# Two copies of an unpacked weight given out later, and Grams, D and lane copies of the steady pairs moved by half a slot or more

## The chip, the cores and the metric

The kernel runs on one core of a Trainium2 chip. The metric is the device time of one launch, in microseconds; lower is better. A core has five engines, each with a queue of its own that it works off in order: TensorE (PE; its weight loads are listed apart as PEld), VectorE (DVE), ScalarE (ACT), GpSimd (POOL) and SyncE (SP, which here only issues DMAs). An instruction starts when its engine comes to it and the semaphores that it waits for have been reached.

## What is computed

The reference is a linear attention by the delta rule, followed by a feed-forward layer. Per batch and head (4 x 8), over 768 steps, with a state matrix of 48 x 48:

```python
for t in range(S):
    y[:, :, t] = np.einsum('bhd,bhde->bhe', q[:, :, t], state)
    v_old = np.einsum('bhde,bhd->bhe', state, kt)
    state = state + bt[:, :, :, None] * np.einsum('bhd,bhe->bhde', kt, vt - v_old)
...
h = x @ w_in
g = np.where(pos, h, np.where(neg, 0.0, (h + beta) ** 2 / (4.0 * beta)))
return (g @ w_out).astype(np.float32)
```

k is normalised, y of the heads side by side is x (3072 tokens x 384), w_in is 384 x 2048 and w_out 2048 x 384; beta of the feed-forward is 1, and pos and neg mean h >= 1 and h <= -1.

## The kernel before

**Chunks and pairs.** The 768 steps are cut into 12 chunks of 64. Two chunks make a pair, so there are 6 pairs, G = 0 to 5. A chunk g is worked on in these pieces, each of them a function that issues matmuls, returns a function that copies the result out (the eviction), and that may return a third part for VectorE:

- `gram(g, i)` (four per chunk): products of keys with keys and of keys with queries, from the loaded tile W. ScalarE copies the first into GG (L150), VectorE masks the second back into W (L163); for the first four chunks ScalarE copies it (L155) and POOL masks it.
- `lanes`: from GG of both chunks, 32 x 32 triangular blocks, one per lane: two generator steps of two copies each (L202), one for each chunk, a transposition (L204), and the norms with gm, ending in the scaling L217 and POOL's mask L218 and memset L220.
- `solve_whole`: 30 steps of two VectorE operations each (L247, L249) that invert the blocks; `unlanes_whole` puts them back (L255, L257, L260). For pairs 0 and 1 `solve` and `unlanes` do it in blocks of 16 (L236, L238, L268 to L272) and `merge16_a` and `merge16_b` put them together.
- `merge32_a` (L308), `merge32_b` (L324): TensorE joins the blocks to 64 x 64. `scale_v` (L184, one VectorE operation for each half of a chunk) multiplies the values by the norm.
- `chain_r` (L338), `chain_u` (L352), `chain_y` (L372), `chain_d` (L396): the chunk's use of the state, its update, its output (split into a high and a low part, L377 to L382, and sent on by six DMAs, L386) and the addition to the state (L407, four VectorE operations). These run chunk after chunk.

**The feed-forward.** For each pair, 16 slices f of the hidden width: `up` (L522, nine matmuls: three slices of the model width times three products of high and low parts), then on ScalarE a Relu from h, a second Relu and a Square (L644, L644, L663), and the max on VectorE (L671); in the next slot's beginning the cast to a high part on ScalarE (`ghi`, L639) and the low part on VectorE (`glo`, L640); two slots later `down` (L537, twelve matmuls). One slice is one slot. Pair 0 has 24 slots (8 of half the tokens, 8 of all, 8 of the other half), the others 16, so 104 in all. `h` has two buffers: an up waits for the max of two slots before. `ch`, which takes the results of the small pieces, has two buffers as well.

**Order.** The order of all instructions is written out by hand. In a slot n come: what is left of the last slot's second half (its evictions); ghi and glo of the last slot; up; first Relu; the pieces that are planned for time n (products); one step of the weight generator `wu`; the fills planned for n; the evictions; another step of `wu`; second Relu, Square; down; the pieces planned for n + 0.5; the max; two steps of `wu`; the fills for n + 0.5. `plan(G)` fills two tables, `pe` for pieces and `fill` for generators and loads, counted from the pair's first slot; a = 2G + 2 and b = 2G + 3 are the chunks of the next pair, whose lanes, solve, merges and chain run beside this pair's feed-forward, while Grams and loads of the pair after it stand near the pair's end. T is 5 for G = 0 and 1 for the steady pairs G = 1 to 4. So in a steady pair chain_y(b) is given out at 14.5, load_w(b + 2) at 15, Grams of a + 2 at 15 and 15.5, of b + 2 at 15.5 and 16, chain_d(b) at 17, which is slot 1 of the next pair, and load_kv(b + 2) at 17.5. W and KV have four buffers, two chunks: load_w(b + 2) has to wait until chain_y(b) has read W, load_kv(b + 2) until chain_d(b) has read KV.

**The weights.** They come as 64-bit words and are unpacked once, tile by tile (16 tiles f), by the generator `weight(f)`, in six steps: a scaling copy on ScalarE (L125), a shift on VectorE (L127), two bit operations on VectorE (L129, L131), the cast to the high part on ScalarE (L135) and the low part on VectorE (L137). `unpack` interleaves the tiles, and each `yield` of it is one step of `wu`: 26 are used before the first slot, then four per slot until slot 9. Four buffers (`X4`) hold the tile in work.

Of the kernel before, what the change touches and what calls it, by code (L numbers as in the profile page):

```python
# [20 lines left out]
FT = DF // 128  # L21
# [8 lines left out]
def delta_rule_moe(ctx: ExitStack, tc: tile.TileContext, kqa, kqb, kv, beta, w, out):  # L30
# [89 lines left out]
    def weight(f):  # L120

        x = X4[:, f % 4]
        st = RAW.pop(f)
        sti, xi = st.bitcast(I32), x.bitcast(I32)
        nc.scalar.mul(out=x, in_=st[:, :, 1::2], mul=2.0 ** -112)  # L125
        yield
        nc.vector.tensor_scalar(out=xi, in0=xi, scalar1=3, scalar2=None, op0=ALU.logical_shift_left)  # L127
        yield
        nc.vector.scalar_tensor_tensor(out=xi, in0=sti[:, :, 1::2], scalar=-0x80000000, in1=xi, op0=ALU.bitwise_and, op1=ALU.bitwise_or)  # L129
        yield  # L130
        nc.vector.scalar_tensor_tensor(out=xi, in0=sti[:, :, 0::2], scalar=29, in1=xi, op0=ALU.logical_shift_right, op1=ALU.bitwise_or)  # L131
        yield
        WT[f] = const.tile([P, 2, 2, DM], F32R, name=f"wt{f}")
        hi, lo = (WT[f][:, :, i, :] for i in range(2))
        nc.scalar.copy(out=hi, in_=x)  # L135
        yield
        nc.vector.tensor_tensor(out=lo, in0=x, in1=hi, op=ALU.subtract)  # L137
        yield


    def gram(g, i):

        w_, us = W[g, i // CT], [i % CT * NP + p for p in range(NP)]
        gp = ps.tile([P, NP, 2, C], F32, **acc())
        for p, u in enumerate(us):
            nc.tensor.matmul(gp[0:C, p], w_[C:C + D, 0, u, :], w_[C:C + D, 0:2, u, :], start=True, stop=True)  # L146
            nc.tensor.matmul(gp[C:P, p], w_[0:D, 0, u, :], w_[0:D, 0:3:2, u, :], start=True, stop=True)  # L147

        def evict():
            nc.scalar.copy(out=GG[:, g % 2, i * NP:(i + 1) * NP], in_=gp[:, :, 0, :])  # L150

            def raw():
                for r, s in ((0, 1), (C, 2)):
                    x = w_[r:r + C, s, us[0]:us[0] + NP]
                    nc.scalar.copy(out=x, in_=gp[r:r + C, :, 1, :])  # L155
                    nc.gpsimd.affine_select(out=x, in_=x, pattern=[[0, NP], [1, C]], base=0, channel_multiplier=-1,
                                            compare_op=ALU.is_gt, fill=0.0)
            if g < 4:
                return raw

            def masks():
                for r, s in ((0, 1), (C, 2)):
                    nc.vector.tensor_tensor(out=w_[r:r + C, s, us[0]:us[0] + NP], in0=gp[r:r + C, :, 1, :],  # L163
                                            in1=mask[r:r + C, None, :].broadcast_to([C, NP, C]), op=ALU.mult)
            return masks
        return evict
# [13 lines left out]
    def scale_v(g):  # L180

        for i in range(NT):
            v, u = KV[g, i][:, 1], g % 2 * NU + i * NV
            nc.vector.tensor_tensor(out=v, in0=v, in1=S["N"][:, u:u + NV, None].broadcast_to([P, NV, D]), op=ALU.mult)  # L184
            yield
# [44 lines left out]
    def solve():  # L230

        X, A16 = S["X"], S["A16"]
        for j in range(15):
            n, m = j + 1, 15 - j
            pr = sb.tile([P, 240], F32, name="pr", bufs=1)[:, 0:2 * n * m].rearrange("l (s c t) -> l s c t", s=2, t=m)
            nc.vector.tensor_tensor(out=pr, in0=X[:, :, 0:n, j:j + 1].broadcast_to([P, 2, n, m]),  # L236
                                    in1=A16[:, :, j:j + 1, j + 1:16].broadcast_to([P, 2, n, m]), op=ALU.mult)
            nc.vector.tensor_tensor(out=X[:, :, 0:n, j + 1:16], in0=X[:, :, 0:n, j + 1:16], in1=pr, op=ALU.subtract)  # L238
            yield
# [177 lines left out]
    def products(*pieces):  # L417
        return [p() for p in pieces]

    def both(f, g):  # L420
        return [lambda i=i: f(g, i) for i in range(NT)]
# [6 lines left out]
    def unpack():  # L428

        gens = [weight(f) for f in range(FT)]  # L430

        def step(f):
            if f < FT:
                next(gens[f])
        step(0)
        step(1)
        for f in range(FT + 2):
            if f < FT:
                step(f)
                yield  # L440
            if f > 1:
                step(f - 2)
                yield
            step(f + 2)
            if f < FT:
                step(f)
                yield
                step(f)
                step(f)
                yield  # L450


    def stage(pieces, *fill):
# [4 lines left out]

    spare += START
    wu, sv, ln, raws = unpack(), [scale_v(0), scale_v(1)], lanes(0), []  # L460
    for g in range(2):
        for i in range(CB):
# [84 lines left out]
    pe, fill = {}, {}  # L547

    def at(where, G, t, *x):
        where.setdefault(2 * first[G] + int(round(2 * t)), []).extend(x)  # L550

    def grams(G, t, g, dt=0.5):
        for j in range(2):
            at(pe, G, t + j * dt, *[lambda i=2 * j + x: gram(g, i) for x in range(2)])

    def plan(G):

        a, b = 2 * G + 2, 2 * G + 3
        if G < NS - 1:
            ln, so, un, va, vb = lanes(G + 1), solve(), unlanes(), scale_v(a), scale_v(b)  # L560
        if G == 0:
            at(pe, G, 0, *both(chain_y, 1))
            at(fill, G, 1, (load_w, 3))
            at(pe, G, 1, *both(chain_d, 1))
            at(fill, G, 1.5, (load_kv, 3))
            grams(G, 2, a)
            grams(G, 4, b)
            at(fill, G, 4, (ln, 1))
            at(fill, G, 5, (ln, 1))
            at(fill, G, 5.5, (ln, 1))  # L570
            at(fill, G, 6, (ln, 9))
            for j in range(8):
                at(fill, G, 6.5 + j / 2, (so, 2))
            at(fill, G, 9, (va, 1))
            at(fill, G, 9.5, (va, 1))
            at(fill, G, 10.5, (un, 1))
            at(fill, G, 11, (un, 9))
            at(fill, G, 13, (vb, 1))
            at(fill, G, 14, (vb, 1))
            T = 5  # L580
        elif G < NS - 1:
            so, un = solve_whole(), unlanes_whole()
            for j in range(2):
                at(fill, G, 2 + j, (va, 1))
                at(fill, G, 11 + j, (vb, 1))
            at(fill, G, 0.5, (ln, 2))
            at(fill, G, 1, (ln, 1))
            at(fill, G, 1.5, (ln, 9))
            cost, H = 0, 0
            for j in range(1, 31):  # L590
                at(fill, G, 2.5 + H / 2, (so, 1))
                cost += j * (31 - j) + 150
                H = int(cost / 9461 * 14)
            for j in range(4):
                at(fill, G, 9.5 + j // 2 / 2, (un, 1))
            T = 1
        if G < NS - 1:
            if G == 0:
                for j, f in enumerate((merge16_a, merge16_b, merge32_a, merge32_b)):
                    for g in range(2):  # L600
                        at(pe, G, T + 7 + j + g / 2, lambda f=f, g=g: f(g))
            else:
                for j, f in enumerate((merge32_a, merge32_b)):
                    for g in range(2):
                        at(pe, G, 10.5 + j + g / 2, lambda f=f, g=g: f(g))
            at(pe, G, T + 6.5, *both(chain_r, a))
            at(pe, G, T + 11, *both(chain_u, a))
            at(pe, G, T + 11.5, *both(chain_y, a))
            at(pe, G, T + 12, *both(chain_d, a))
            at(pe, G, T + 12.5, *both(chain_r, b))  # L610
            at(pe, G, T + 13, *both(chain_u, b))
            at(pe, G, T + 13.5, *both(chain_y, b))
            if G < NS - 2:
                at(fill, G, T + 12, (load_w, a + 2))
                at(fill, G, T + 12.5, (load_kv, a + 2))
                late = 0 if G == 0 else 2
                at(pe, G, T + 14 + late, *both(chain_d, b))
                at(fill, G, T + 14, (load_w, b + 2))
                at(fill, G, T + 14.5 + late, (load_kv, b + 2))
                grams(G, T + 14 + (G == 0) / 2, a + 2)  # L620
                grams(G, T + 14.5 + (G == 0), b + 2)

    for G in range(NS):
        plan(G)
# [21 lines left out]
    late, last, ready = [], None, []  # L646
    for n, item in enumerate(items):
# [22 lines left out]
        late = products(*pe.pop(H + 1, []))  # L670
# [6 lines left out]
    G = NS - 1  # L677
# [50 lines left out]
```

## Time and profile before

| | us |
|---|---|
| three runs | 716.6, 718.3, 722.27 (median 718.3) |
| profiled execution, its own time | 714.19 |
| its span, first to last instruction | 712.2 |
| TensorE's granted clock, mean of the span | 0.944 |

In the profile, times count from the first instruction. The stretch before the first slot ends near 80 us, pair 0's slots lie between 80 and 230, the steady pairs 1 to 4 take some 97 to 106 us each (the first up of pairs 2, 3 and 4 stands near 328, 432 and 537), and pair 5, which has only its feed-forward, begins near 634. A group of instructions is named by its line, its engine and its tiles (out<-in); "idle before" is the time in which the engine had nothing running ahead of it, and the arrow names what ended that time.

### The profile page before, as it was taken

To read this page: it belongs to the slowest core of one execution; us is meant where nothing else is said; L and a number is where in the kernel's file an instruction comes from. 1 tells how busy PE (TensorE), PEld (TensorE's weight loads), DVE (VectorE), ACT (ScalarE), POOL (GpSimd) and SP (SyncE) were. 2 spreads that over 40 slices of the span, in tenths; PEclk is the share of its full clock that TensorE was granted. 3 is DMA by queue.
4 is the path that set the end of the run, shared out by engine and by line. 5 is a ranking of instruction groups with operands and counts; after the bars stand their busy time and mean duration, and the time that the engine had idled before them with its cause. 6 is when DMAs were issued, how large, how long until landed. Compare 5 with 4: busy or idle time off the path is not lost.

```text
span 712.2 us, 19365 instructions
## 1 busy us (share of the span) xinstructions
PE 646.0 (91%) x8428; PEld 558.4 (78%) x8428; DVE 440.7 (62%) x920; ACT 400.1 (56%) x720; POOL 45.1 (6%) x90
## 2 busy tenths in 40 slices
PE   8848776679999899998999999999989999999996
PEld 7348775468898788887888878888878888889985
DVE  2857667894255798346996445996436996433332
ACT  3327666454845565844467653457554467556663
POOL 3212022001000200000200000200000200000000
PEclk9955988799999999999999998999998999999999
DMA  8960430000053000042300150300150200001001
GB/s 235 417 252 9 118 99 1 0 1 5 3 137 103 23 1 1 5 112 59 89 1 2 34 121 20 88 2 2 39 133 10 83 1 2 14 13 44 1 1 45
DMA packets 18532, 41.45 MB, mean 58 GB/s; under 512 B 3600, under 2 KB 9104, under 8 KB 18448
## 3 DMA queue, kind: packets, MB, share of 16 engines
q1 hardware_dynamic: 18112, 40.04, 19.5%
q8 instruction: 66, 1.08, 0.6%
q14 instruction: 18, 0.15, 0.1%
q0 software_dynamic: 256, 0.08, 0.1%
q10 hardware_dynamic: 80, 0.10, 0.1%
HBM read 33.13 MB, written 4.72 MB: 53 GB/s over the span
## 4 chain that ended last, share of the span: by engine, by line
PE 47%; DVE 33%; ACT 6%; issue 5%; DMA 4%; SPq 3%; DVEq 0%; ACTq 0%
PE h L522 15%; PE o L537 14%; DVE pr L247 5%; DVE A L249 4%; DVE s L671 4%; DVE glo L640 4%; DMA W<-in_kqa_dram 3%; PE ch L372 3%; PE ch L352 3%; SPq L386 2%; PE ch L146 2%; PE ch L324 2%; PE ch L396 2%; PE ch L308 2%; PE ch L338 2%
## 5 line engine op out<-in xcount | busy, mean ns | idle before, releaser
L522 PE MATMUL h<-xb,wt 128*128 128x512 f32 (+1 forms) x936 | 231.8, 393 | 13.6 <-DVE s L671 11.4
L522 PEld LDWEIGHTS h<-xb,wt 128*128 128x128 f32 x936 | 167.9, 194 | 52.2 <-DVE s L671 16.6
L537 PE MATMUL o<-wt,ghi 128*128 128x384 f32 x768 | 202.0, 344 | 2.4 <-ACT ghi L639 2.4
L537 PEld LDWEIGHTS o<-wt,ghi 128*128 128x128 f32 x768 | 138.1, 189 | 11.6 <-ACT ghi L639 3.0
L671 DVE TENSOR_TENSOR s<-h,s 128x512 f32<-128x512 f32 (+1 forms) x104 | 66.9, 643 | 113.9 <-ACT s L663 113.8
L537 PE MATMUL o<-wt,glo 128*128 128x384 f32 x384 | 131.6, 343 | 2.4 <-DVE glo L640 2.1
L639 ACT CAST ghi<-s 128x512 fp32r<-128x512 f32 (+1 forms) x104 | 61.1, 588 | 94.5 <-DVE s L671 68.6
L644 ACT ACTIVATE s<-h,half 128x512 f32<-128x512 f32 (+1 forms) x104 | 67.9, 653 | 56.7 <-PE h L522 56.3
L640 DVE TENSOR_TENSOR glo<-s,ghi 128x512 fp32r<-128x512 f32 (+1 forms) x104 | 67.3, 647 | 44.6 <-ACT ghi L639 44.2
L537 PEld LDWEIGHTS o<-wt,glo 128*128 128x128 f32 x384 | 72.6, 189 | 6.0 <-DVE glo L640 6.0
L644 ACT ACTIVATE s<-s,one 128x512 f32<-128x512 f32 (+1 forms) x104 | 71.9, 691 | 2.9
L663 ACT ACTIVATE s<-s 128x512 f32<-128x512 f32 (+1 forms) x104 | 62.3, 599 | 3.3
L146 PE MATMUL ch<-W 48*64 48x128 f32 x336 | 47.8, 300 | 17.7 <-DMA W<-in_kqa_dram 7.0
L146 PEld LDWEIGHTS ch<-W 48*64 48x64 f32 x336 | 42.3, 150 | 23.4 <-issue 13.9
L147 PE MATMUL ch<-W 48*64 48x128 f32 x336 | 48.0, 300 | 0.0
L163 DVE TENSOR_TENSOR W<-ch,mask 64x256 f32<-64x256 f32 x64 | 27.0, 422 | 32.6 <-ACT GG L150 31.7
L249 DVE TENSOR_TENSOR A<-A,pr 128x30 f32<-128x30 f32 (+14 forms) x120 | 39.8, 332 | 4.4
L147 PEld LDWEIGHTS ch<-W 48*64 48x64 f32 x336 | 42.2, 150 | 0.0
L247 DVE TENSOR_TENSOR pr<-A 128x30 f32<-128x30 f32 (+14 forms) x120 | 39.3, 328 | 2.2
L150 ACT COPY GG<-ch 128x256 f32<-128x256 f32 x42 | 15.2, 372 | 37.2 <-PE ch L147 37.1
L218 POOL TENSOR_SCALAR_AFFINE_SELECT A<-A 128x1024 f32<-128x1024 f32 x4 | 6.4, 1593 | 370.4 <-DVE A L217 370.4
L135 ACT CAST wt<-xb 128x768 fp32r<-128x768 f32 x16 | 13.3, 832 | 28.9 <-DVE xb L131 28.9
(137 smaller groups left out, 721.1 us busy)
## 6 DMA issues: line engine op xcount, KB each, us to landing
wt<-in_w_dram SPq DMA_DIRECT2D x16, 768.0 KB, 13.7
KV<-in_kv_dram SPq DMA_DIRECT2D x24, 384.0 KB, 5.5
W<-in_kqb_dram SPq DMA_DIRECT2D x24, 256.0 KB, 4.7
W<-in_kqa_dram SPq DMA_DIRECT2D x24, 192.0 KB, 4.9
out_dram<-wx SPq DMA_DIRECT2D x47, 96.0 KB, 2.2
xb<-X SPq DMA_DIRECT2D x66, 32.0 KB, 2.0
xb<-A SPq DMA_DIRECT2D x6, 32.0 KB, 2.0
beta_sb<-in_beta_dram POOLq DMA_DIRECT2D x8, 10.0 KB, 2.4
```

The source lines that it names most:

```text
L146: nc.tensor.matmul(gp[0:C, p], w_[C:C + D, 0, u, :], w_[C:C + D, 0:2, u, :], start=True, stop=True)
L147: nc.tensor.matmul(gp[C:P, p], w_[0:D, 0, u, :], w_[0:D, 0:3:2, u, :], start=True, stop=True)
L163: nc.vector.tensor_tensor(out=w_[r:r + C, s, us[0]:us[0] + NP], in0=gp[r:r + C, :, 1, :], in1=mask[r:r + C, None, :].broadcast_to([C, NP, ...
L247: nc.vector.tensor_tensor(out=pr, in0=A[:, 0:n, j:j + 1].broadcast_to([P, n, m]), in1=A[:, j:j + 1, j + 1:32].broadcast_to([P, n, m]), op= ...
L249: nc.vector.tensor_tensor(out=A[:, 0:n, j + 1:32], in0=A[:, 0:n, j + 1:32], in1=pr, op=ALU.add)
L522: nc.tensor.matmul(h[:, cols(bs)], WT[f][:, 0, x, k * P:(k + 1) * P], XB[G][:, y, k, cols(bs)], start=(n == 0), stop=(n == 8))
L537: nc.tensor.matmul(oacc[G, k], (ghi, glo)[x][:, k * P:(k + 1) * P], WT[f][:, 1, y, :], start=(new and n == 0), stop=(left[G, b] == 0 and n ...
L639: nc.scalar.copy(out=ghi[:, c], in_=s[:, c])
L640: nc.vector.tensor_tensor(out=glo[:, c], in0=s[:, c], in1=ghi[:, c], op=ALU.subtract)
L644: nc.scalar.activation(out=out, in_=in_, func=AF.Relu, bias=bias, scale=scale)
L663: nc.scalar.activation(out=s[:, c], in_=s[:, c], func=AF.Square)
L671: nc.vector.tensor_tensor(out=s[:, c], in0=h[:, c], in1=s[:, c], op=ALU.max)
```

## The change

Two edits. In `unpack`, the step that makes the high part of tile f (L135, together with the second bit operation in one step of `wu` before) is taken one tile later, ahead of the second bit operation of tile f + 1; and the scaling copy of tile f + 2 (L125), which stood ahead of the first bit operation of f, comes behind the last step of f.

In `plan`, for the steady pairs:

- scale_v of chunk a: from 2 and 3 to 4 and 5;
- lanes: from two steps at 0.5, one at 1, the rest at 1.5, to one step each at 0.5, 1 and 1.5 and the rest at 2;
- chain_d(b) from 17 to 15, load_kv(b + 2) from 17.5 to 15.5 (G = 1 to 3);
- Grams of b + 2 from 15.5 and 16 to 16 and 16.5 (G = 1 to 3).

chain_r(a) is written in another place with the same times (11.5 for G = 0, 7.5 for the steady pairs), and G = 0 keeps its times. Number and size of all instructions stay.

```diff
@@ -441,13 +441,15 @@
             if f > 1:
                 step(f - 2)
                 yield
-            step(f + 2)
             if f < FT:
                 step(f)
                 yield
-                step(f)
+            if 0 < f <= FT:
+                step(f - 1)
+            if f < FT:
                 step(f)
                 yield
+            step(f + 2)
...
@@ -581,11 +583,12 @@
             for j in range(2):
-                at(fill, G, 2 + j, (va, 1))
+                at(fill, G, 4 + j, (va, 1))
                 at(fill, G, 11 + j, (vb, 1))
-            at(fill, G, 0.5, (ln, 2))
+            at(fill, G, 0.5, (ln, 1))
             at(fill, G, 1, (ln, 1))
-            at(fill, G, 1.5, (ln, 9))
+            at(fill, G, 1.5, (ln, 1))
+            at(fill, G, 2, (ln, 9))
...
         if G < NS - 1:
+            at(pe, G, 11.5 if G == 0 else 7.5, *both(chain_r, a))
...
-            at(pe, G, T + 6.5, *both(chain_r, a))
...
@@ -613,12 +617,11 @@
-                late = 0 if G == 0 else 2
-                at(pe, G, T + 14 + late, *both(chain_d, b))
+                at(pe, G, T + 14, *both(chain_d, b))
                 at(fill, G, T + 14, (load_w, b + 2))
-                at(fill, G, T + 14.5 + late, (load_kv, b + 2))
+                at(fill, G, T + 14.5, (load_kv, b + 2))
                 grams(G, T + 14 + (G == 0) / 2, a + 2)
-                grams(G, T + 14.5 + (G == 0), b + 2)
+                grams(G, T + 15 + (G == 0) / 2, b + 2)
```

## The prediction

> **What bounds the kernel now.** I read the page first (busy shares), then busy time by stretches, then the timelines of single engines in the two stretches that the edits touch, and the chain of work that ended last for the joints between pairs.
>
> ```profile
> PE 646.0 (91%) x8428; PEld 558.4 (78%) x8428; DVE 440.7 (62%) x920; ACT 400.1 (56%) x720; POOL 45.1 (6%) x90
> 80.00:158.00 78.00, 54.28 (x435) 45.71 (x435) 59.30 (x119) 44.96 (x92) 9.97 (x21) 0.80 0.15 39
> 441.00:489.00 48.00, 46.62 (x386) 40.52 (x386) 45.63 (x106) 26.39 (x42) 3.83 (x6) 1.00 0.12 34
> ```
>
> TensorE looks like the bound at 91%, but not everywhere. In 80 to 158 us, where pair 0's feed-forward starts and the weights are still unpacked, it works 54 of 78 us and part of that at a low clock (0.80 mean); VectorE works 59, ScalarE 45, and neither is full: they wait for each other. In 441 to 489 us, a steady pair's solve, VectorE has 45.6 of 48 and TensorE 46.6: there the two are level, and what one gains the other has to gain too. Elsewhere TensorE alone sets the pace.
>
> (A row of the second view has start and end of the stretch, its length, the busy time of PE, PEld, DVE, ACT and POOL, the granted clock, and the DMAs.) How the waiting looks in the first stretch, on VectorE's timeline (start, duration, instruction, in brackets the idle time before it and what ended it):
>
> ```profile
> 85.23 0.42 DVE L671 TENSOR_TENSOR s<-h,s 128x256 f32<-128x256 f32 x1
> ...
> 86.55 0.96 DVE L131 SCALAR_TENSOR_TENSOR xb<-wt,xb 128x768 int32<-128x768 int32 x1
> 88.71 0.43 DVE L640 TENSOR_TENSOR glo<-s,ghi 128x256 fp32r<-128x256 f32 x1 [1.20 <-ACT ghi L639]
> ...
> 92.71 0.41 DVE L671 TENSOR_TENSOR s<-h,s 128x256 f32<-128x256 f32 x1
> ...
> 99.49 0.42 DVE L671 TENSOR_TENSOR s<-h,s 128x256 f32<-128x256 f32 x1 [1.55 <-ACT s L663]
> ...
> 107.24 0.41 DVE L671 TENSOR_TENSOR s<-h,s 128x256 f32<-128x256 f32 x1
> ...
> 114.03 0.42 DVE L671 TENSOR_TENSOR s<-h,s 128x256 f32<-128x256 f32 x1 [0.36 <-ACT s L663]
> ...
> 122.40 0.42 DVE L671 TENSOR_TENSOR s<-h,s 128x256 f32<-128x256 f32 x1
> ```
>
> and ScalarE in two slots of it:
>
> ```profile
> 95.01 0.83 ACT L135 CAST wt<-xb 128x768 fp32r<-128x768 f32 x1 [1.29 <-DVE xb L131]
> ...
> 99.04 0.42 ACT L663 ACTIVATE s<-s 128x256 f32<-128x256 f32 x1
> 99.36 0.89 ACT L125 ACTIVATE xb<-wt 128x768 f32<-128x768 f32 x1
> 101.80 0.84 ACT L135 CAST wt<-xb 128x768 fp32r<-128x768 f32 x1 [1.55 <-DVE xb L131]
> ...
> 106.23 0.42 ACT L663 ACTIVATE s<-s 128x256 f32<-128x256 f32 x1
> ```
>
> A slot ends with the max (L671). VectorE then does the weight's two bit operations (L129 and L131, 0.96 each, 86.55 for the second); ScalarE's second copy (L135) stands in its queue ahead of the slot's cast ghi (L639), though that cast needs only the max. So ScalarE idles 1.29 to 1.55, copies 0.83, casts, and VectorE's glo (L640) idles 1.20 for it. The order is a ring, and each turn pays both halves.
>
> **The change, part by part.** *Unpacking.* Counted over its yields, the copy of weight f now comes one weight later, ahead of f+1's second bit operation, and the first copy (L125) half a slot later, after that operation. Number of instructions and yields stay. When its turn comes, the copy's input is a slot old: it runs right behind the Square, while VectorE does max and bit operations (0.42 + two times 0.96), and 0.83 + 0.40 of ScalarE fit under that. Slot by slot (max to max, from the rows, before 7.48, 6.78, 7.75, 6.79, 8.37):
> - first: VectorE-bound, loses its wait of 1.20: 6.28.
> - second to fifth carry the Grams' copies, so ScalarE becomes the bound. Its own work there is 95.01 to 99.46, 4.45 for a slot with the Gram inside, 101.80 to 106.65, 4.85 for one with the Gram behind it, plus 0.89 for L125: 5.35 and 5.75 without waits. The second slot begins with its copy done (minus 0.74 net): 4.6, which the bit operations and glo stretch to about 5.1; third 5.75; fourth 5.4; fifth 6.2, since there VectorE's lane copies and low part come after the late ghi.
> - sixth and later: other VectorE work (lane copies, transposition, solve) already covers the copy: no change.
>
> Saved 1.2 + 1.7 + 2.0 + 1.4 + 2.2 = 8.5. TensorE runs behind the max there and follows. Below, the bound is 4 (three waits of 1.20, one more, if Grams at half clock hold ScalarE back); above 9.5.
>
> Ahead of the loop the same copies stand on the chain of waits, directly before copies that TensorE waits for (L314, L401, L356; start, share of the chain, what):
>
> ```profile
> 55.64 0.83 ACT wt L135
> ...
> 70.40 0.80 ACT xb L125
> ...
> 77.73 0.83 ACT wt L135
> ```
>
> Three times 0.8, but at each place the copy behind has another wait close by (TensorE's own issue, the next DMA), and L125 now lands ahead of a y cast once (0.9 against). Bounds -2.5 and +0.9; I take -0.8, one of the three.
>
> *Joints between steady pairs.* chain_d(b) moves from slot 17 to 15, KV's load with it on SP's queue (from behind the output stores to right behind W's), Grams b half a slot later (16, 16.5).
>
> ```profile
> 423.92 4.18 DMA W<-in_kqa_dram
> ...
> 428.24 0.44 PE L146 MATMUL ch<-W 48*64 48x128 f32 x1 [2.15 <-DMA W<-in_kqa_dram]
> ...
> 424.49:427.90 3.41, 1.61 (x30) 1.36 (x26) 1.69 (x4) 0.74 (x2) 0.00 (x0) 1.00 0.96 213
> 427.90:434.73 6.83, 6.49 (x39) 5.61 (x40) 2.38 (x5) 1.26 (x3) 0.00 (x0) 0.50 0.14 30
> ...
> 325.92 0.29 PE L146 MATMUL ch<-W 48*64 48x128 f32 x1 [1.79 <-DMA W<-in_kqa_dram]
> ...
> 327.89 2.29 PE h L522 x9
> ```
>
> Gram b waits for W's DMA 2.15 us; TensorE was busy 1.61 of the 3.41 us before 427.90, and then its clock is 0.50 for 6.83 us, which costs some 3.4 more. The joint before (1.79 of waiting) kept its clock. After, chain_d (64 small matmuls, 1.57 from its start at 301.22 to the down behind it, 302.79) and an up (2.29) stand between the earlier Grams and this one, 3.9 us against 2.15: the wait goes, and the half clock with it. KV's two loads land behind W's on the same queue; W's second tile is needed some 6 us later than its issue would land, so I cost that at nothing; without that cover, up to the 2.15 again.
>
> But the joint is not TensorE's alone. From chain_y(b)'s end to merge32_a's start:
>
> ```profile
> 313.74 2.04 PE ch L372 x64
> ...
> 345.17 1.23 DVE A L217
> ...
> 382.82 1.20 PE ch L308 x63
> ...
> 415.71 2.04 PE ch L372 x64
> ...
> 437.40 2.31 PE o L537 x12
> ...
> 450.50 1.23 DVE A L217
> ...
> 488.16 1.20 PE ch L308 x63
> ...
> 521.12 2.04 PE ch L372 x64
> ...
> 593.83 1.20 PE ch L308 x63
> ```
>
> These are from the chain; the timelines of VectorE and POOL add what lies around L217:
>
> ```profile
> 249.72 0.55 DVE L184 TENSOR_TENSOR KV<-KV,N 128x384 f32<-128x384 f32 x1
> ...
> 302.19 2.28 DVE L407 TENSOR_TENSOR SU<-ch,SU 48x384 f32<-48x384 f32 x4 [1.12 <-PE ch L396]
> ...
> 346.53 1.59 POOL L218 TENSOR_SCALAR_AFFINE_SELECT A<-A 128x1024 f32<-128x1024 f32 x1 [97.87 <-DVE A L217]
> ...
> 442.08 2.00 DVE L204 STREAM_TRANSPOSE A<-GG 128x1024 f32<-128x1024 f32 x1
> ...
> 452.25 1.60 DVE L184 TENSOR_TENSOR KV<-KV,N 128x384 f32<-128x384 f32 x1
> ...
> 454.37 0.17 DVE L247 TENSOR_TENSOR pr<-A 128x30 f32<-128x30 f32 x1
> ```
>
> From L372's end to L308 it takes 67.0, 70.4 and 70.7, and in the first two the part from L217's end to merge32_a is 36.4 (346.40 to 382.82, 451.73 to 488.16): VectorE without a gap. It sets the end. The new stretch: TensorE, to the end of slot 17's up, has three ups (2.29 each, 6.9), chain_d (1.6), four pairs of Grams (1.97 each, 325.92 to 327.89: 7.9), two downs (2.31 each, 4.6), and a wait: the first Gram takes the buffer that chain_d(b) held until L407's first two additions are over, about 0.55, and 0.2 for the second. Sum 21.6. Then down (2.3) and VectorE's run from transposition to L217's end, 9.65 before (442.08 to 451.73); out of it go L407 (2.28) and one of the two store copies (0.5), which comes while down runs, and glo comes in (0.6): 9.8 with the down. L217 ends at 31.4. From there the scale_v (1.60, beside POOL's 1.59) no longer lies before the solve: the solve starts at +2.0 (POOL's 1.59, its memset and the hand-overs) instead of +2.64 (451.73 to 454.37), and scale_v costs 0.55 later: 36.3. Merge32_a at 67.7: +0.7, -2.7, -3.0 against the three. The joint from pair 0 has no chain_d or Gram moved, only lanes and scale_v: glo (0.6) comes earlier, scale_v later, -2.64 + 2.0 + 0.6 + 0.55: +0.5. Together -4.5. Bounds: if TensorE were the bound again, the three would be some 3 lower each (-13.5); if nothing but the new costs acted, +2.
>
> chain_r(a) is given out at the same slots as before, 11.5 and 7.5; pair 0's joint Grams too: no cost.
>
> Sum: -8.5 - 0.8 - 4.5 = -13.8 on the profiled execution's 714.2 us: 700.4. The runs' median is 718.3, 4.1 above that execution, so the forecast for the median is 704.5.
>
> **A rule against it.** The granted clock fell after a stretch with 1.61 of 3.41 us busy (row above). The Trainium skill, TensorE: Matmul & The Clock Gate, Part 1 (The HAM clock gate), has the clock fall after at least one idle window of about 3.4 us. By that rule a wait of 2.15 would not be the cause, and the half clock would stay; this trace disagrees, since no window before 427.90 was idle throughout.
>
> **The rivals.**
> - *Half clock stays* at both joints, whatever removes the wait: the -2.7 and -3.0 go, 710.2. Against it: the fall at 427.90 ends the very window that holds the W wait, and the joint with 1.79 has none. (The clock page's rule would have it so.)
> - *Grams bind pair 0.* TensorE's Grams at half clock hold ScalarE's copies, so that only the bare waits of 1.20 go: 4 instead of 8.5, 709. For it: clock 0.80 in that stretch.
> - *TensorE is the bound after all* in the joints, VectorE finds room: up to 9 lower, 695.5. Against it: the constant 36.4.
> - *Slower: the solve starts late.* Lane copies half a slot later push L217 back by x beyond my 31.4 at all four joints, TensorE idles in front of merge32_a, and once over half of a 3.41 us window is idle its clock halves for 6.83 us, another 3.4. Then 4x + 13.6 - 13.8: over 1% slower from x = 1.85, less than the half slot (a slot is 4 to 5 us) that they are moved; at 2.5 it gives 728. Against it: these copies fit in before VectorE must wait for slot 17's Square anyway.
> - *No effect*: another engine ends every one of these waits at the same time: 718.
>
> **How the numbers follow.** Forecast 0.62 (its own range 699 to 709), half clock stays 0.07, Grams bind 0.12, TensorE bound 0.08, slower 0.05, no effect 0.06. The range 695.5 to 711 takes in the first four. About 1% (7.2 us) is what a measurement of this kernel can tell from no change: faster 0.86, same 0.09, slower 0.05.
>
> **What would show it.** Right: between 80 and 135 us L135 no longer waits for L131 and L640 not 1.20; the max that ends slot 5 (122.40 now) comes some 9 us earlier. No wait of L146 for W at the joints, clock 1.00 there; chain_y(b) to merge32_a near 67.7 in all. A short wait of the first Gram for L407. Wrong: merge32_a waiting over 2 us for L257, a clock of 0.50 at a joint, or L671 waiting as before for the Square.

## The result, and the profile after

| | before | after |
|---|---|---|
| runs, median (us) | 718.58 (four, 716.6 to 722.27) | 695.43 (four, 694.46 to 695.97) |
| profiled execution, its own time | 714.19 | 695.40 |
| its span | 712.2 | 693.4 |

The ratio is 0.9671, with a 95% interval from 0.963 to 0.9711: faster, by 23 us, where 14 were forecast. The direction and both mechanisms held; the distance that was added between one execution and the median did not, and the time fell just under the low end of the range. (One run of the experiment e2_plan, 2246.79 us, was disturbed and is left out everywhere below.)

Line numbers after the edit are three higher than before: the max is L674, glo L643, ghi L642, the Square L666.

The page of the changed kernel, busy times of the whole span, and two of its stretches with the columns of the prediction's rows: start and end, length, busy PE, PEld, DVE, ACT, POOL, then the granted clock. The first is the stretch 80 to 158 of before, moved with the loop's start; the second is the first half of a joint.

```profile
PE 637.4 (92%) x8428; PEld 552.6 (80%) x8428; DVE 437.2 (63%) x920; ACT 397.7 (57%) x720; POOL 44.8 (6%) x90
```

```profile
77.50:155.50 78.00, 60.98 (x775) 52.82 (x775) 64.75 (x126) 49.69 (x101) 11.03 (x21) 0.86 0.16 42
...
304.00:335.40 31.40, 30.74 (x296) 26.64 (x295) 22.76 (x50) 14.66 (x29) 0.00 (x0) 1.00 0.34 87
```

The same 78 us now hold 61.0 us of TensorE work (54.3 before) and 64.8 of VectorE work (59.3): more of the same work in the same time, and idle time gone.

VectorE's timeline of the changed kernel over the first slots (start, duration, instruction; in brackets the idle time before it and what ended it):

```profile
82.78 0.42 DVE L674 TENSOR_TENSOR s<-h,s 128x256 f32<-128x256 f32 x1
...
88.97 0.41 DVE L674 TENSOR_TENSOR s<-h,s 128x256 f32<-128x256 f32 x1
...
93.99 0.43 DVE L674 TENSOR_TENSOR s<-h,s 128x256 f32<-128x256 f32 x1 [0.85 <-ACT s L666]
...
97.24 0.52 DVE L643 TENSOR_TENSOR glo<-s,ghi 128x256 fp32r<-128x256 f32 x1 [0.97 <-ACT ghi L642]
...
99.41 0.42 DVE L674 TENSOR_TENSOR s<-h,s 128x256 f32<-128x256 f32 x1
...
104.55 0.42 DVE L674 TENSOR_TENSOR s<-h,s 128x256 f32<-128x256 f32 x1
...
108.51 0.54 DVE L643 TENSOR_TENSOR glo<-s,ghi 128x256 fp32r<-128x256 f32 x1 [1.52 <-ACT ghi L642]
...
111.16 0.42 DVE L674 TENSOR_TENSOR s<-h,s 128x256 f32<-128x256 f32 x1
```

and ScalarE's:

```profile
81.65 0.42 ACT L666 ACTIVATE s<-s 128x256 f32<-128x256 f32 x1
81.97 0.82 ACT L135 CAST wt<-xb 128x768 fp32r<-128x768 f32 x1
83.23 0.41 ACT L642 CAST ghi<-s 128x256 fp32r<-128x256 f32 x1 [0.44 <-DVE s L674]
...
93.86 0.82 ACT L135 CAST wt<-xb 128x768 fp32r<-128x768 f32 x1
```

L135 no longer waits for L131: it follows the Square directly, and ghi follows the max at once. In the first, second and fourth slots glo doesn't wait at all; the waits left (0.97 in the third, 1.52 in the fifth) come in the slots in which ScalarE copies two Grams ahead of ghi. From max to max it is 6.19, 5.02, 5.42, 5.14 and 6.61, together 28.38, where it was 37.17.

The joints, from the chain of work that ended last (start, duration, engine, out, line, count); L372 is the end of chain_y(b), L308 the start of merge32_a:

```profile
194.53 2.02 PE ch L372 x64
...
269.11 1.20 PE ch L308 x63
...
302.00 2.02 PE ch L372 x64
...
334.17 1.24 DVE A L217
...
371.09 1.20 PE ch L308 x63
...
404.00 2.02 PE ch L372 x64
...
473.08 1.20 PE ch L308 x63
...
505.99 2.02 PE ch L372 x64
...
575.09 1.20 PE ch L308 x63
```

The joint from pair 0 takes 72.56 (196.55 to 269.11; 72.27 before), the three others 67.07 each, all alike, where they were 67.06, 70.44 and 70.69. What TensorE's Grams waited for from 300 to 560 us (engine, line, what for, us in total, times, longest), first before, then after:

```profile
PE ch L146 <- DMA W<-in_kqa_dram: 6.3, 3, 2.3
```

```profile
PE ch L146 <- PE ch L396: 1.7, 3, 0.6
```

The wait for W is gone at all three. What is left is the Gram that follows chain_d(b) directly, as these two rows of the changed kernel's timelines show:

```profile
307.22 2.28 DVE L407 TENSOR_TENSOR SU<-ch,SU 48x384 f32<-48x384 f32 x4 [1.12 <-PE ch L396]
```

```profile
308.44 0.29 PE L146 MATMUL ch<-W 48*64 48x128 f32 x1 [0.55 <-PE ch L396]
```

The second of L407's four additions ends half way through the group, near 308.35, and the Gram starts 0.1 later. So the wait of 0.55 is for VectorE, though the row names the matmuls, which had ended at 307.89.

Added up from the landmarks of the two profiled executions (before to after): start to the first max -2.45, slots 0 to 5 -8.79, from there to chain_y(b) of pair 0 -0.78, the joints +0.29, +0.02, -3.37 and -3.61, all else under 0.1: -18.8, the difference of the spans. The medians differ by 23.15, 4.4 more than the two executions' own times. Where those come from is the first question for the experiments, the parts of the change the second.

### The profile page after: what moved, and what is told of

It is laid out like the page before. It is cut to its first block, busy times and chain, and to the rows that moved or that the text cites. A ratio compares the mean times of both kernels' runs of the same rounds, so it can differ in the third digit from the quotient of the medians.

```text
span 693.4 us, 19365 instructions
## 1 busy us (share of the span) xinstructions
PE 637.4 (92%) x8428; PEld 552.6 (80%) x8428; DVE 437.2 (63%) x920; ACT 397.7 (57%) x720; POOL 44.8 (6%) x90
## 4 chain that ended last, share of the span: by engine, by line
PE 54%; DVE 29%; ACT 6%; issue 5%; DMA 2%; SPq 2%; POOL 1%; DVEq 0%; POOLq 0%; ACTq 0%
PE o L539 17%; PE h L524 16%; DVE pr L247 5%; DVE A L249 4%; PE ch L146 4%; DVE glo L643 4%; PE ch L372 3%; DVE s L674 3%; PE ch L352 3%; PE ch L324 2%; PE ch L396 2%; DVE A L204 2%; PE ch L308 2%; DMA W<-in_kqa_dram 2%; PE ch L338 2%
## 5 line engine op out<-in xcount | busy, mean ns | idle before, releaser
L674 DVE TENSOR_TENSOR s<-h,s 128x512 f32<-128x512 f32 (+1 forms) x104 | 67.0, 644 | 112.9 <-ACT s L666 112.5
L642 ACT CAST ghi<-s 128x512 fp32r<-128x512 f32 (+1 forms) x104 | 61.3, 589 | 110.4 <-DVE s L674 81.4
L643 DVE TENSOR_TENSOR glo<-s,ghi 128x512 fp32r<-128x512 f32 (+1 forms) x104 | 67.1, 645 | 36.3 <-ACT ghi L642 35.9
L666 ACT ACTIVATE s<-s 128x512 f32<-128x512 f32 (+1 forms) x104 | 62.3, 599 | 3.3
L146 PE MATMUL ch<-W 48*64 48x128 f32 x336 | 43.1, 278 | 9.3 <-ACT W L155 3.7
L146 PEld LDWEIGHTS ch<-W 48*64 48x64 f32 x336 | 37.2, 136 | 14.9 <-issue 5.5
L147 PE MATMUL ch<-W 48*64 48x128 f32 x336 | 43.4, 279 | 0.0
L147 PEld LDWEIGHTS ch<-W 48*64 48x64 f32 x336 | 37.2, 136 | 0.0
L218 POOL TENSOR_SCALAR_AFFINE_SELECT A<-A 128x1024 f32<-128x1024 f32 x4 | 5.1, 1265 | 365.4 <-DVE A L217 365.4
L407 DVE TENSOR_TENSOR SU<-ch,SU 48x384 f32<-48x384 f32 x40 | 22.2, 555 | 9.2 <-PE ch L396 8.5
```

Of the source, the lines that this page charges most:

```text
L642: nc.scalar.copy(out=ghi[:, c], in_=s[:, c])
L643: nc.vector.tensor_tensor(out=glo[:, c], in0=s[:, c], in1=ghi[:, c], op=ALU.subtract)
L666: nc.scalar.activation(out=s[:, c], in_=s[:, c], func=AF.Square)
L674: nc.vector.tensor_tensor(out=s[:, c], in0=h[:, c], in1=s[:, c], op=ALU.max)
```

## The experiments

Each comparison is with the kernel before, run on the same chip between the runs of the experiment (medians of before: 716.49 for e3 to e4_hi, 715.48 for e4b, e8, e9 and e6, 717.59 for e7 and e11 to e13).

### The kernel before once more (e3_before)

No edit.

> The kernel before once more, for a second profile. Theory: its executions differ in how many joints drop to half clock (two in the first profile, 0.50 for 6.83 us each); an execution of 718 has one or two stretches of 0.50 more, at the first or second joint, and there the up and Gram matmuls take nearly double. Rival: the same two stretches of 0.50, and the time lies elsewhere.

Measured: 712.9 (ten runs, 710.17 to 719.29), ratio 0.9975 [0.9937, 1.0012]. Its profiled execution took 718.97, and the joints 71.50, 70.25 and 71.64 (chain_y(b) ends at 315.32, 421.79 and 526.99, merge32_a starts at 386.82, 492.05 and 598.63). The wait of its Grams, and stretches around the first and third joint:

```profile
PE ch L146 <- DMA W<-in_kqa_dram: 8.3, 3, 3.4
```

```profile
323.32:326.73 3.41, 0.37 (x8) 0.15 (x5) 1.64 (x4) 0.37 (x1) 0.00 (x0) 1.00 0.99 209
326.73:333.56 6.83, 6.82 (x40) 5.82 (x41) 2.38 (x5) 1.26 (x3) 0.00 (x0) 0.50 0.01 2
...
534.99:538.40 3.41, 0.37 (x8) 0.13 (x4) 1.64 (x4) 0.37 (x1) 0.00 (x0) 1.00 1.00 214
538.40:545.20 6.80, 6.45 (x39) 5.57 (x40) 2.38 (x5) 1.26 (x3) 0.00 (x0) 0.50 0.13 29
```

This time the clock is 0.50 behind all three waits, the first joint's among them, and that joint is 4.4 us longer than in the execution on which the prediction was built. The reason is in the chain, where the DMA that the Gram waits for has a duration of its own at each joint:

```profile
321.52 5.09 DMA W<-in_kqa_dram
...
427.99 3.89 DMA W<-in_kqa_dram
...
534.20 4.41 DMA W<-in_kqa_dram
```

How late W lands changes from joint to joint and from run to run, and the time with it. Of these ten executions, the five with a mean granted clock of 0.946 or more took 710.17 to 712.23, the five at 0.933 to 0.944 took 713.56 to 719.29. The five profiles of kernels with this part unchanged (before, e3, e1, e4_hi, e4b) have 15 such joints, and 14 of them had the half clock, 13 for 6.8 us and one (the first of e1) for 3.4. The one without it is the first joint of the first profile.

### The two edits alone (e1_unpack, e2_plan)

e1_unpack has the whole edit of `unpack` and the plan as before:

```diff
-            step(f + 2)
             if f < FT:
                 step(f)
                 yield
-                step(f)
+            if 0 < f <= FT:
+                step(f - 1)
+            if f < FT:
                 step(f)
                 yield
+            step(f + 2)
```

> The kernel before with the unpacking edit alone. Theory (the two edits act at places of their own and add): the max that ends slot 5 comes 10.5 to 11.5 us earlier than the 122.40 of before, merge32_a of the first joint about 12 earlier, joints as before (67.0 to 70.7 from chain_y(b) to merge32_a), so 718.6 - 12 = 706.6, and runs still spread over some us. Rival (the saved time is given back, since TensorE or a later wait takes over): slot 5 earlier, but less than 6 us left at the first joint, 712 or more.

Measured: 705.27 (703.43 to 708.5), ratio 0.9841 [0.9801, 0.9881]. Slots 0 to 5 take 29.06. The joints are those of before, as expected: 69.85, 70.47, 71.13, all with the half clock, and its Grams waited 8.2 us for W.

e2_plan has the plan's edits and `unpack` as before:

```diff
-                at(fill, G, 2 + j, (va, 1))
+                at(fill, G, 4 + j, (va, 1))
...
-            at(fill, G, 0.5, (ln, 2))
+            at(fill, G, 0.5, (ln, 1))
             at(fill, G, 1, (ln, 1))
-            at(fill, G, 1.5, (ln, 9))
+            at(fill, G, 1.5, (ln, 1))
+            at(fill, G, 2, (ln, 9))
...
-                at(pe, G, T + 14 + late, *both(chain_d, b))
+                at(pe, G, T + 14, *both(chain_d, b))
-                at(fill, G, T + 14.5 + late, (load_kv, b + 2))
+                at(fill, G, T + 14.5, (load_kv, b + 2))
-                grams(G, T + 14.5 + (G == 0), b + 2)
+                grams(G, T + 15 + (G == 0) / 2, b + 2)
```

> The kernel before with the edits of plan alone (Grams, D, KV's load, lanes, scale_v). Theory: pair 0 as before, each joint 67.1 from chain_y(b) to merge32_a with no clock of 0.50 there, span about 712.2 - 7 = 705, and, if the 4.4 us by which the runs before lie above their profiled execution are further half-clock windows at the joints, these go too: median 707, runs within 1.5 us of each other. Rival (those 4.4 us are a cost outside the joints): median 711.5 and a spread as before.

Measured: 705.87, 707.8 and 708.44, ratio 0.9871 [0.9847, 0.9895]. Slots 0 to 5 take 37.20, the joints 67.09, 67.07 and 67.08, the one from pair 0 71.98. The joints are as expected. So the two edits act apart: 11.2 from `unpack`, about 8.7 from the plan. The sum, 19.9, is some 3 us short of what both brought together; the runs of before alone, which enter all these differences, spread over more than that.

### Which copy counts (e4_hi_only, e4b_mul_only)

e4_hi_only moves L135 alone, e4b_mul_only L125 alone:

```diff
-                step(f)
+            if 0 < f <= FT:
+                step(f - 1)
+            if f < FT:
                 step(f)
```

```diff
-            step(f + 2)
             if f < FT:
...
+            step(f + 2)
```

> The kernel before with only the cast to the high part (L135) given out a tile later, the scaling copy (L125) where it was. Theory (the cast's wait in ScalarE's queue is the whole of it): 8.5 to 11 us earlier at the end of slot 5, 707 to 710 in all; the state copies L401 still stand behind L125, so up to 1 less than both. Rival (L125 also waits, for L137, 9.6 us in all, and has to move too): less than 5 us.

> The kernel before with the scaling copy (L125) alone given out later, the cast (L135) in its old place. Theory: the ring of max, bit operations, cast, ghi, glo is untouched, so slots 0 to 5 shorten by less than 1.5 us: 715 to 718. Rival (L125's waits for L137, 9.6 us in all, delay ScalarE as well): 3 us or more off slots 0 to 5.

Measured: L135 alone 707.33 (706.78 to 708.22), 0.9872 [0.9855, 0.9888], slots 0 to 5 in 29.81. L125 alone 718.08 (709.8 to 720.73), 1.0008 [0.9968, 1.0048], slots 0 to 5 in 38.89, 1.7 longer than unedited, where less than 1.5 shorter was expected. VectorE's timeline of e4b_mul_only still has glo waiting behind the late copy:

```profile
86.43 0.42 DVE L640 TENSOR_TENSOR glo<-s,ghi 128x256 fp32r<-128x256 f32 x1 [1.20 <-ACT ghi L639]
...
103.72 0.53 DVE L640 TENSOR_TENSOR glo<-s,ghi 128x256 fp32r<-128x256 f32 x1 [3.42 <-ACT ghi L639]
```

The ring was L135 behind L131 and ahead of ghi. Moving L125 brings nothing by itself, and some 1 us on top of L135's move (28.0 to 29.1 in the six kernels with both).

### The plan's pieces (e8_d_only, e9_grams_only, e6_lanes)

e8_d_only moves only chain_d(b) and KV's loads:

```diff
-                late = 0 if G == 0 else 2
+                late = 0
```

> The kernel before with chain_d(b) and KV's load alone moved to 15 and 15.5; Grams, lanes and scale_v as before. Theory: chain_d's 1.6 us and the first Gram's wait for L407 lie ahead of Grams b, so W's wait (1.8 to 3.4 us before) shrinks to at most 1.2 and no joint drops to half clock; joints 66.5 to 68, about 708 in all, as with all edits of plan. Rival (the half slot of Grams b is what hides W): over 1.5 us of waiting left and 0.50 at one joint or more, 712 or above.

Measured: 702.34 (701.91 to 703.65), 0.9805 [0.9767, 0.9844]: where 708 was expected, and more than all of the plan's edits together. No wait for W, no half clock, and joints of 66.10, 66.12 and 66.12, a whole us shorter than in the changed kernel.

e9_grams_only leaves chain_d(b) at 17 and makes the other three moves (Grams b, lanes, scale_v, as in e2_plan's diff).

> The kernel before with Grams b half a slot later and the lane and scale_v times that go with it, chain_d(b) and KV's load at 17 and 17.5 as before. Theory: an up of 2.3 us stands ahead of Grams b, W's wait falls to at most 1.2, no half clock, but L407 (2.3 us) stays in VectorE's run ahead of the transposition, so joints are 68 to 69.5: 710 to 713. Rival (VectorE's order does not matter, the W wait is all): joints 67 as with all edits, 708.

Measured: 705.41 (704.16 to 706.32), 0.9845 [0.9812, 0.9877], joints 66.61, 66.14 and 66.16; one wait of 0.40 for W is left, and no half clock. The expected length of 68 to 69.5 fell, and the 710 to 713 with it. Either move takes the wait away; with both, the joint is a us longer than with one.

e6_lanes makes only the moves of lanes and scale_v.

> The kernel before with lane copies, transposition, norms and scale_v alone given out later. Theory: W's wait and the half clock stay, each joint changes by less than 1 us either way; 716 to 718, no difference that can be told. Rival (late lanes push the solve back by half a slot): joints 2 us longer, 722 or more.

Measured: 713.34 (ten runs, 709.47 to 720.91), 0.998 [0.9939, 1.0021]. No difference by itself; the waits for W stay at 2.1 to 2.2 us. But the half clock, which was expected to stay, came at one joint only: the joints take 68.07, 69.75 and 68.03.

### Scale_v back (e7_va_back)

The changed kernel, with

```diff
-                at(fill, G, 4 + j, (va, 1))
+                at(fill, G, 2 + j, (va, 1))
```

> The changed kernel with scale_v of set a back at half slots 2 and 3, all else as changed. Theory: scale_v (L184) falls beside GpSimd's L218 again; each takes about 1.6 us there in place of 0.55 and 1.27, and from L217's end to merge32_a it is 36.3 to 36.4 us again in place of 35.7, so each of four joints is 0.6 to 0.7 us longer: joints of 67.7, about +2.5 us, 698. Rival: the move of scale_v prices nothing (the 0.7 us came from the lane copies): joints stay at 67.1, 695.4.

Measured: 695.12 (693.78 to 695.35), 0.9684 [0.9656, 0.9712], joints 67.08: as changed. The theory fell. VectorE's timeline shows why, and POOL's below it:

```profile
331.24 0.54 DVE L184 TENSOR_TENSOR KV<-KV,N 128x384 f32<-128x384 f32 x1
...
334.38 1.23 DVE L217 SCALAR_TENSOR_TENSOR A<-A,gm 128x1024 f32<-128x1024 f32 x1
335.52 0.68 DVE L674 TENSOR_TENSOR s<-h,s 128x512 f32<-128x512 f32 x1
...
339.73 0.55 DVE L184 TENSOR_TENSOR KV<-KV,N 128x384 f32<-128x384 f32 x1
```

```profile
335.74 1.27 POOL L218 TENSOR_SCALAR_AFFINE_SELECT A<-A 128x1024 f32<-128x1024 f32 x1 [98.26 <-DVE A L217]
```

With the lanes half a slot later, L217 lies behind one scale_v and before the other. Neither meets L218, and each costs its 0.55. So with the lanes moved, moving scale_v as well adds nothing.

### What beats the change (e11_unpack_d, e12_scale_v, e13_store)

e8 said that the Grams should stay. e11_unpack_d is e1_unpack with e8's one line. e12_scale_v adds scale_v at 4 and 5 (first hunk of e2_plan's diff). e13_store adds:

```diff
-            (nc.scalar.copy, nc.vector.tensor_copy)[k % 2](out=o[:, k % 2], in_=oacc[G, k])
+            (nc.scalar.copy if G < NS - 1 else (nc.scalar.copy, nc.vector.tensor_copy)[k % 2])(out=o[:, k % 2], in_=oacc[G, k])
```

> The kernel before with the unpack edit and, of the plan, only chain_d of set b and its K/V loads moved early; Grams, lane copies and scale_v where they were. Theory: no wait for W, no half clock and no Gram ahead of its diagonal: joints of 66.1 us as with D alone (67.1 in the changed kernel), slots 0 to 5 at 28.4: about 692.5, 3 us under the changed kernel. Rival: the quicker unpack starts the solve at another moment and the Gram order matters then: joints of 67 or more, 695 or more.

> The run before this one (unpack edit, chain_d of set b early) and scale_v of set a at half slots 4 and 5. Theory: L218 alone takes 1.27 us and L217's end to merge32_a 35.7: four joints shorter by 0.6 to 0.7 us, 65.4 to 65.5, about 690. Rival: the lane copies at their old places hold L217's follower in another way, and nothing is won: 692.5.

> The run before this one and both copies of the output tile (L543) on ScalarE in all pairs but the last. Theory: VectorE's run ahead of the solve is what binds the joint still, and is shorter by 0.5 to 1 us: joints of about 64.7, 687. Rival: ScalarE's copies of the hi part (L407's neighbours) come later for it and the joint keeps its length or grows: 690 to 692.

| | median, range | ratio | steady joints | joint from pair 0 |
|---|---|---|---|---|
| e11 | 691.63, 690.41 to 694.65 | 0.9647 [0.9614, 0.9681] | 66.16, 66.17, 66.14 | 72.24 |
| e12 | 690.81, 689.19 to 692.6 | 0.963 [0.9601, 0.966] | 65.76, 65.76, 65.75 | 72.33 |
| e13 | 689.11, 686.89 to 689.78 | 0.9601 [0.9574, 0.9628] | 65.33, 65.32, 65.31 | 71.73 |

One joint of each, in the chain of work that ended last, e11, e12 and e13 in turn:

```profile
299.95 2.02 PE ch L372 x64
...
330.46 1.23 DVE A L217
...
368.13 1.20 PE ch L308 x63
```

```profile
303.24 2.02 PE ch L372 x64
...
333.75 1.24 DVE A L217
...
371.01 1.20 PE ch L308 x63
```

```profile
301.74 2.02 PE ch L372 x64
...
331.82 1.24 DVE A L217
...
369.08 1.20 PE ch L308 x63
```

All three stand below the changed kernel. e11 came as expected. In e12, L217 ends where it ended in e11 (29.7 after chain_y(b)), and merge32_a follows 36.0 after it in place of 36.4: 0.4 where 0.6 to 0.7 were expected, because glo still lies beside L218, as it does in e11; in the changed kernel it comes later. The timelines of VectorE and of POOL show it (in these three kernels, glo is L642 and the max L673):

```profile
334.89 0.68 DVE L642 TENSOR_TENSOR glo<-s,ghi 128x512 fp32r<-128x512 f32 x1
335.49 0.68 DVE L673 TENSOR_TENSOR s<-h,s 128x512 f32<-128x512 f32 x1
```

```profile
335.11 1.59 POOL L218 TENSOR_SCALAR_AFFINE_SELECT A<-A 128x1024 f32<-128x1024 f32 x1 [96.55 <-DVE A L217]
```

In e13, where joints of 64.7 and 687 were expected, L217 ends 0.4 earlier, half of what the two copies took from VectorE (0.98 in all). The rest came back as a wait of 0.80 for ScalarE's y, which now stands behind the four copies, in place of 0.30. In each kernel the joint still goes through L217. Between neighbours of the table, the runs overlap; the joints carry these steps, the medians only their sum.

## Why the prediction was right, and where it was not

**The offset: the step that failed.** "The runs' median is 718.3, 4.1 above that execution, so the forecast for the median is 704.5." I treated the difference between one execution and the median as a constant that any kernel would carry. The changed kernel doesn't carry it: its median (695.43) is its profiled time (695.40). In the unedited kernel, time goes with the granted clock (e3's ten executions), and at least part of that lies at the joints which the change mends: e3's profiled execution is 4.8 longer than the first, and its three steady joints are 5.2 longer. In the first profile the first joint kept its clock; in 14 of the 15 such joints profiled it didn't. The three steady joints add up to 208.2 in that profile and to 211.5 on the mean of the five profiles of e3's section. The changed kernel has 201.2 (the same in e7), its waits being gone. So against the mean, the three joints' term was not -5.0 (0.7 - 2.7 - 3.0) but -10.3, and nothing was to be added back. The rows to see it by were in the prediction itself: 1.79 and 2.15 us of waiting for one DMA, with a clock kept at the one and lost at the other, and a median that lay above.

Not all of the 4.1 is placed by this. The four runs of before in the first comparison have no traces, and the median of before is itself a draw: 718.58 there, 712.9 for e3's ten, 715.48 to 717.59 in the other sets. With the joints at -10.3, the slots at -8.8, the start at -1.4 and the stretch behind the slots at -0.8 (the last two by the means below), some 21 of the 23 us are accounted for; the other 2 are less than those medians differ by.

**Unpacking.** -8.5 was forecast for slots 0 to 5; -8.8 came, slot by slot within 0.4: 6.28, 5.1, 5.75, 5.4 and 6.2 against 6.19, 5.02, 5.42, 5.14 and 6.61. That the ring was L135's is shown by e4_hi_only and e4b_mul_only. The rival of Grams at half clock that bind pair 0 (4 us) fell.

**Ahead of the loop.** -0.8, with bounds of -2.5 and +0.9. One pair of profiles says -2.45, which is not to be trusted: the first max stands at 81.97 to 85.23 in seven kernels with L135 where it was, mean 83.5, and at 81.32 to 82.78 in seven with it moved, mean 82.1. That is -1.4. From slot 5 to chain_y(b) of pair 0, where no change was forecast, the means are 86.9 and 86.1, with ranges that overlap.

**Joints: the parts.** L217's end was worked out at 31.4 after chain_y(b), and comes at 31.38 (304.02 to 335.40). (The terms of its first part add up to 21.7, where the prediction has 21.6.) The wait for L407 was to be 0.55 and 0.2; it is 0.55 and 0.1. From L217 to merge32_a it is 35.7 instead of 36.3: L218 takes 1.27 where I counted its 1.59, and the solve doesn't wait for the memset behind it. That makes 67.07 for 67.7, and +0.3, or nothing, for the +0.5 of the joint from pair 0 (e3's unedited one takes 72.52). But I had put this gain down to scale_v's move, and by e7 it is there without that move, with the lanes later.

**What the sum missed by.** 704.5 less 695.4 is 9.1: 4.1 is the offset, 2.2 the four joints against the first profile, 1.6 the start (mostly its scatter), 0.3 the slots, 0.8 the stretch behind them, and 0.1 rounding.

**The rivals.** The half clock didn't stay, and the solve started late nowhere. The time lies by that of "TensorE is the bound after all", but its mechanism isn't what gave it: the joints are 67.1, not 3 lower than 67.7, and the chain goes through L217 in all four. In the first part TensorE is full (30.74 of 31.40 us in the row above), in the second, from L217's end to merge32_a, VectorE is busy for 33.2 of 35.7 us and its operations make up the chain, as the sum had it.

**The plan as a whole.** Of its pieces chain_d(b) and KV's loads alone carry the gain (e8); the other moves, made on top of it, give a us per joint back. L217's end comes 31.4 after chain_y(b), in e8 29.7; 0.7 of that returns behind it, where L218 is left alone. VectorE's timeline of the changed kernel shows what L217 waits for: the transposition, half a slot later, now stands behind the max and the store copies, which wait 0.61 and 0.50 for a down:

```profile
327.76 0.56 DVE L545 COPY wx<-o 128x384 f32<-128x384 f32 x1 [0.50 <-PE o L539]
...
328.95 2.05 DVE L204 STREAM_TRANSPOSE A<-GG 128x1024 f32<-128x1024 f32 x1
```

So it starts 24.9 after chain_y(b)'s end, in e8 22.3, where the store copies come behind it and wait for nothing. The late Grams and the late lanes were not tried apart beside the early chain_d(b). In e9, with chain_d(b) at 17, L217 ends at 30.5: the first pair of Grams doesn't wait for L407 (0.55) and takes 1.96 instead of 2.29. That is 0.8 later than in e8, and 0.7 less follows, which is why the two are equally quick.

## What to carry to other kernels

- The distance between one profiled execution and the median can belong to a stretch that the change touches. Profile the unchanged kernel more than once before it is carried over as a constant, above all where a wait for a DMA lies near the edge at which the clock falls.
- In a ring of two engines, find the one instruction whose input comes late and which stands ahead of the short step that the other engine needs. Giving out that one later brought most of the gain (9.2 of 11.2 us); moving its neighbour alone brought nothing.
- When a wait is removed by putting work ahead of it, try the smallest such move first: one line (e8) did better than four moves.

## What the runs showed of the hardware

**The clock.** In all fourteen traces the granted clock is 1.00 or 0.50, and every stretch between two changes lasts a whole number of 3.41 us (3.41, 6.83, 10.24 and so on). So the clock can be followed window by window, counted from its changes. Six profiled kernels wait about 1.8 us or more for W at each of the three steady joints (the five of e3's section and e6_lanes), 18 joints in all. At 15 the clock fell to 0.50, behind windows in which TensorE was busy 0.37 us (e3) to 1.86 (e4_hi_only); at three it stayed at 1.00, and the windows have 2.03 (the first joint of before), 2.14 and 2.12 (the first and third of e6_lanes). The kept one of before, then one kept and one lost in e6_lanes (the rows' columns are those of the stretches above):

```profile
322.10:325.51 3.41, 2.03 (x33) 1.72 (x32) 1.98 (x5) 0.74 (x2) 0.00 (x0) 1.00 0.80 172
...
322.59:326.00 3.41, 2.14 (x33) 2.00 (x34) 1.06 (x4) 0.51 (x2) 0.00 (x0) 1.00 0.56 125
...
424.99:428.40 3.41, 1.42 (x26) 1.45 (x28) 1.05 (x3) 0.48 (x2) 0.00 (x0) 1.00 0.76 159
```

The three waits of e6_lanes are alike (2.12, 2.22 and 2.08). All but 0.2 of the second lies inside one window; the two others are cut by a window's end, at 322.59 and at 530.80. So it isn't the wait's length alone, but where it lies in the window. Nor is busy time the whole rule: in the joint from pair 0, the clock of e1_unpack stayed at 1.00 behind a window with 1.70 (232.58 to 235.99), and why is open.

The Trainium skill, TensorE: Matmul & The Clock Gate, Part 1 (The HAM clock gate), asks for an idle window before the fall. The traces differ: no window at these joints was wholly idle, and the clock fell behind 15 of 18. Its window of about 3.4 us that runs on by itself agrees with the stretches of 3.41 us and their multiples.

**VectorE and POOL beside each other.** L218 takes 1.27 with only the max beside it, and 1.59 beside scale_v or glo; scale_v takes 0.55 alone and 1.60 beside L218, glo 0.68 either way. The Trainium skill, GPSIMD Engine Reference, 1. Specifications, has the two engines share their way to SBUF, with contention where VectorE reads two inputs from there. This agrees: scale_v and glo read two tiles from SBUF, while the max takes h from PSUM. The sizes, 0.3 on the one side and 1.05 on the other, are from the rows.
